# A weighted mixture kernel on one core: probabilities moved into the second product's operands, weight sums moved to other steps

## The chip, the core and the metric

The kernel runs on one core of one Trainium2 chip. The metric is device time in microseconds (us) of one execution, the median of three runs. Lower is better.

## The reference

Four sequences of 576 tokens, 8 heads of 64 columns, give 2304 tokens of 512 columns. Linear attention with an RMS norm makes `x`; a gated layer of 2048 hidden columns follows; then a mixture of four experts, which is what the change touches:

```python
p = domain_probs / (domain_probs.sum(-1, keepdims=True) + 1e-09)
for e in range(4):                       # w1[e]: 512 x 1024, w2[e]: 1024 x 512
    h = np.maximum(x @ w1[e], 0.0)
    out += p[:, e:e + 1] * (h @ w2[e])
```

## The kernel before

The first 468 us of the profiled execution are attention and the gated layer; the change leaves them alone but for the early part of the mixture's first operands. The rest is class `Second`. It walks 24 steps: three tiles of 768 tokens (tile 1, 2 and 3), and in each the eight half experts of 512 hidden columns. Step n has a first product (512 x 512 weights times 512 x 768 tokens) and a second product of the same size. fp32 is kept by splitting each operand into a rounded high part and a remainder: ScalarE (ACT) copies the high part (`split`, L158), VectorE (DVE) or GpSimd (POOL) subtracts it from the operand (L159). A product is then three matmul terms.

Each product is done on 2 x 2 blocks. The first product always, and the second from step 8 on, uses seven block products in place of eight, with sums of blocks as operands: `sumw` sums weight blocks, `sumx` tokens, `sumh` hidden values. A block product is 12 matmuls on TensorE (PE). In tile 1 weights come raw from memory (`load1`, `load2`), are split there, written to a buffer in HBM (`put_away`) and read back from it in tiles 2 and 3 (`get`); in tile 1 the second product has eight plain blocks (`second`), two block products for each of the four outputs.

`events` gives every action a time slot; one slot is one block product. Sorting by slot makes the program, and each engine runs its part strictly in order. A step has 15 slots in tile 1 and 14 later; first products of step n stand on odd slots, second products of step n-1 on even ones, so PE always has one of the two. All DMAs of this part but the middle outputs leave from one queue, SP's.

First products accumulate in two PSUM tiles, `x` and `z`. `keep` (ACT) and `add` (DVE, L267) move partial results to SBUF tiles `f`, named c11, c12, c22; the fourth block, c21, is what is left in `x` at the end. From these the second product's operands `hid` are made: in tile 1 by `hid` (ACT relu, L278, then a DVE subtraction with relu, L279), one for each c; later by `relu`, `sumh`, `oph`. Blocks of the second product are then multiplied by the token's probability and added to `acc`: in tile 1 by `weigh` (DVE multiplies out of PSUM, L324; POOL adds, L326), later by `keep_o`, `add`, `weigh_o` (ACT copies out of PSUM, DVE adds the next partial result, POOL multiplies, L352, and adds, L354). `leave` transposes finished tokens of tiles 1 and 2 on PE, one small piece in each of six later steps, in a bank of `ox`; `leave_last` does tile 3.

Of the kernel before, what the change touches and what calls it, by code (L numbers as in the profile page):

```python
# [80 lines left out]
class Second:  # L81
# [15 lines left out]
    ORDER = (0, 3, 2, 4, 5, 6, 1)  # L97
# [7 lines left out]
    def __init__(self, tc, w, acc, p_dram, w_dram, ident, out):  # L105
        self.tc, self.nc = tc, tc.nc
        self.w, self.acc, self.p_dram, self.w_dram, self.ident, self.out = w, acc, p_dram, w_dram, ident, out
        self.steps = NP * E2
        self.start = [0]
        for n in range(self.steps):  # L110
            self.start.append(self.start[-1] + (self.LONG if n <= E2 else self.SHORT))
        self.stacks = {}
        self.x, self.w1, self.w2, self.raw, self.s, self.h, self.f, self.t, self.ps, self.pb = ({} for _ in range(10))
# [16 lines left out]
    def open_left(self):  # L130
# [6 lines left out]
        self.m_p = self.open("left", "m", 2)  # L137
        self.away_p = self.open("first_left", "away", 2)
        self.s2_p = self.open("first_left", "s2", 3)
        self.raw2_p = self.open("first_left", "raw2", 4)  # L140
        self.ps2 = self.open("psum", "ps2", 1, space=PSUM)

    def change(self):

        self.stacks["first_right"].close()
        self.stacks["first_left"].close()
        self.t_p = self.open("right", "t", 6, side="right")
        self.h7_p = self.open("right", "hid7", 1, side="right")
        self.e_p = self.open("left", "e", 4)
# [124 lines left out]
    def hid(self, n, name, src):  # L274

        src = self.f[n, src] if src in ("c11", "c12", "c22") else self.of_ps(n, src)
        h = self.hid_tile(name)
        self.nc.scalar.activation(h[:, 0], src, AF.Relu)  # L278
        self.nc.vector.scalar_tensor_tensor(h[:, 1], src, 0.0, h[:, 0].bitcast(F32), op0=ALU.max, op1=ALU.subtract)  # L279
        self.h[n, name] = h  # L280

    def relu(self, n, name):
        self.nc.scalar.activation(self.f[n, name], self.f[n, name], AF.Relu)

    def sumh(self, n, name):

        f = self.t_p.tile([128, 2, HN], F32, tag="t", name="t")
        if name == "t3":
            self.nc.vector.tensor_tensor(f, self.f[n, "t2"], self.f[n, "c11"], op=ALU.subtract)
        else:  # L290
            a, b = dict(t1=("c12", "c11"), t2=("c22", "t1"), t4=("x", "t2"))[name]
            a = self.of_ps(n, a) if a == "x" else self.f[n, a]
            self.nc.vector.scalar_tensor_tensor(f, a, 0.0, self.f[n, b], op0=ALU.max, op1=ALU.subtract)
        self.f[n, name] = f

    def oph(self, n, name, eng=None):
        h = self.hid_tile(name)
        self.split(h, self.f[n, name], eng)
        self.h[n, {"c11": "b11"}.get(name, name)] = h
# [15 lines left out]
    def probs(self, n, j):  # L315
        t, q = divmod(n, E2)
        return self.pb[t, q // 2][:, j * HN : j * HN + HN].unsqueeze(1).to_broadcast([128, 2, HN])

    def weigh(self, n, b):

        i, j = self.BLOCKS[b]
        a = self.sums(0, i, j)
        m = a if n == 0 else self.m_p.tile([128, 2, HN], F32, tag="m", name="m")
        self.nc.vector.tensor_tensor(m, self.of_ps(n, b), self.probs(n, j), op=ALU.mult)  # L324
        if n:
            self.nc.gpsimd.tensor_tensor(a, a, m, op=ALU.add)  # L326
# [8 lines left out]
    def keep_o(self, n, c, name):  # L335
        t = self.e_p.tile([128, 2, HN], F32, tag="e", name="e")
        self.nc.scalar.activation(t, self.of_ps(n, c), AF.Copy)  # L337
        self.f[n, name] = t

    def weigh_o(self, n, name, c=None):  # L340

        i, j = int(name[1]) - 1, int(name[2]) - 1
        a = self.sums(n // E2, i, j)
        fresh, last = n % E2 == 0, n == self.steps - 1
        eng = self.nc.vector if last and name != "o11" else self.nc.gpsimd
        if c:
            m = a if fresh else self.e_p.tile([128, 2, HN], F32, tag="e", name="e")
            self.nc.vector.tensor_tensor(m, self.of_ps(n, c), self.probs(n, j), op=ALU.mult)  # L348
        else:
            t = self.f.pop((n, name))  # L350
            m = a if fresh else t
            eng.tensor_tensor(m, t, self.probs(n, j), op=ALU.mult)  # L352
        if not fresh:
            (self.nc.vector if last and c else eng).tensor_tensor(a, a, m, op=ALU.add)  # L354

    def leave(self, t, b):

        p = self.bank(self.ps2, 0, "t")
# [25 lines left out]
    def events(self):  # L384
# [7 lines left out]
        for n in range(self.steps):  # L392
# [17 lines left out]
            lead = self.LEAD + (2.5 if n == 0 else 0)  # L410
            for k in range(7):
# [24 lines left out]
            put(b0 + 10.5, self.hid, n, "b22", "c22")  # L436
            put(b0 + 12.1, self.add, n, "z", "c12")
            put(b0 + 12.2, self.ps.pop, (n, "z"))
            put(b0 + 14.1, self.hid, n, "b21", "x")
            if make:  # L440
                put(b0 + 4.5, self.hid, n, "b11", "c11")
                put(b0 + 12.5, self.hid, n, "b12", "c12")
                put(b0 + 14.2, self.ps.pop, (n, "x"))
                for i, name in ((4.6, "c11"), (10.6, "c22"), (12.6, "c12")):
                    put(b0 + i, self.f.pop, (n, name))

                for k, (i, j) in enumerate(((0, 0), (0, 1), (1, 0), (1, 1))):
                    put(b0 + (5.6 if n == 1 else 1) + 0.5 * k, self.load2, n, i, j)
                    put(b0 + (7.2, 8.6, 10.2, 14.7)[k] + 0.7 * (n == 1), self.op2, n, f"a{i + 1}{j + 1}", pool)
                for k, i in ((0, 10), (1, 11.5), (6, 17.2)):  # L450
                    put(b0 + i, self.put_away, n, 2, k)
                late = (9, 4)[n] if n < 2 else 0
                for name, i in (("s1", 5.2), ("s2", 5.3), ("s3", 9.2), ("s4", 11.2)):
                    put(b0 + late + i, self.sumw, n, 2, name, pool if name in ("s1", "s3") else None)
                for k, i in ((3, 5.5), (4, 9.4), (2, 11.3), (5, 13.2)):
                    i += late
                    put(b0 + i, self.op2, n, self.A[k], pool if k != 2 else None)
# [523 lines left out]
```

## Time and profile before

| | us |
|---|---|
| median of three runs (1262.45 to 1264.41) | 1262.68 |
| profiled execution | 1257.88 |
| its span, first to last instruction | 1255.4 |
| PE busy in the span | 1191.7 |

The profiled execution is 4.8 us below the median of the runs. The span is read in four stretches: 0 to 468 us (attention and gated layer), 468 to 742 (tile 1), 742 to about 1228 (tiles 2 and 3, with the change of tile at 985 to 1026), and the end. "Busy" of an engine counts its own instructions. An arrow `<-` names what ended an engine's idle time. PEclk is the granted share of TensorE's clock: 1.00 is 2.4 GHz, 0.50 is 1.2 GHz.

### The profile page before, as it was taken

To read this page: it belongs to the slowest core of one execution; us is meant where nothing else is said; L and a number is where in the kernel's file an instruction comes from. 1 tells how busy PE (TensorE), PEld (TensorE's weight loads), DVE (VectorE), ACT (ScalarE), POOL (GpSimd) and SP (SyncE) were. 2 spreads that over 40 slices of the span, in tenths; PEclk is the share of its full clock that TensorE was granted. 3 is DMA by queue.
4 is the path that set the end of the run, shared out by engine and by line. 5 is a ranking of instruction groups with operands and counts; after the bars stand their busy time and mean duration, and the time that the engine had idled before them with its cause. 6 is when DMAs were issued, how large, how long until landed. Compare 5 with 4: busy or idle time off the path is not lost.

```text
span 1255.4 us, 17061 instructions
## 1 busy us (share of the span) xinstructions
PE 1191.7 (95%) x6513; PEld 1111.5 (89%) x6513; DVE 756.1 (60%) x932; ACT 498.6 (40%) x777; POOL 579.5 (46%) x369
## 2 busy tenths in 40 slices
PE   6889999999999998999999979999999899999996
PEld 5778798888888887899999979999999899999996
DVE  4985545555653467667777764455557755555555
ACT  4555443433332244443443333333334433333333
POOL 2563433302300034577766753255556553555553
PEclk9999999999999999999999999999999999999999
DMA  9523011201200028787878666888888678878863
GB/s 331 194 72 110 22 63 51 67 1 52 67 1 1 1 84 288 265 310 283 299 266 296 234 236 233 262 262 260 268 262 253 228 236 258 262 264 262 263 203 100
DMA packets 85235, 234.48 MB, mean 187 GB/s; under 512 B 10204, under 2 KB 32804, under 8 KB 85156
## 3 DMA queue, kind: packets, MB, share of 16 engines
q1 hardware_dynamic: 83140, 230.23, 54.8%
q10 hardware_dynamic: 2016, 3.18, 0.7%
q8 instruction: 51, 0.84, 0.3%
q14 instruction: 28, 0.23, 0.1%
HBM read 169.91 MB, written 63.48 MB: 186 GB/s over the span
## 4 chain that ended last, share of the span: by engine, by line
PE 64%; DVE 9%; issue 5%; ACT 3%; POOL 2%; DMA 2%; SPq 2%; DVEq 0%; POOLq 0%; ACTq 0%
PE a L831 12%; PE p_h L793 12%; PE ps_x L249 12%; PE ps_ox L249 9%; PE ps_z L249 8%; PE ps_oz L249 7%; PE ps_o L312 4%; DVE w L159 2%; DVE f L267 2%; DVE s L200 1%; ACT hid L278 1%; DMA raw<-in_w 1%; SPq L183 1%; ACT w L158 1%; POOL w L159 1%
## 5 line engine op out<-in xcount | busy, mean ns | idle before, releaser
L249 PE MATMUL ps_x<-x,w 128*128 128x384 f32 x1152 | 217.1, 336 | 2.4 <-DVE f L267 2.4
L249 PEld LDWEIGHTS ps_x<-x,w 128*128 128x128 f32 x1152 | 203.1, 189 | 2.8 <-DVE f L267 2.7
L312 PE MATMUL ps_o<-hid,w 128*128 128x384 f32 x768 | 152.5, 347 | 20.3 <-ACT hid L278 20.2
L249 PE MATMUL ps_z<-x,w 128*128 128x384 f32 x864 | 163.3, 337 | 4.3 <-issue 2.2
L312 PEld LDWEIGHTS ps_o<-hid,w 128*128 128x128 f32 x768 | 139.3, 195 | 24.6 <-ACT hid L278 22.8
L249 PEld LDWEIGHTS ps_z<-x,w 128*128 128x128 f32 x864 | 151.7, 189 | 6.5 <-issue 3.3
L249 PE MATMUL ps_ox<-hid,w 128*128 128x384 f32 x768 | 145.4, 337 | 5.3 <-ACT e L337 5.3
L249 PEld LDWEIGHTS ps_ox<-hid,w 128*128 128x128 f32 x768 | 135.1, 189 | 6.2 <-ACT e L337 6.2
L793 PE MATMUL p_h<-x_hi,w_hi 128*128 128x512 f32 (+1 forms) x320 | 119.9, 375 | 1.1 <-ACT o L729 1.1
L653 POOL TENSOR_TENSOR cv_a<-wd_raw,cv_a 128x512 f32<-128x512 f32 x28 | 37.6, 1341 | 180.4 <-ACT sg L807 71.2
L793 PE MATMUL p_h<-x_lo,w_hi 128*128 128x512 f32 (+1 forms) x320 | 119.1, 372 | 0.5 <-DVE x_lo L779 0.5
L831 PE MATMUL a<-h_lo,w_hi 128*128 128x512 f32 (+1 forms) x320 | 118.3, 370 | 1.1 <-DVE h_lo L817 1.1
L793 PE MATMUL p_h<-x_hi,w_lo 128*128 128x512 f32 (+1 forms) x320 | 119.0, 372 | 0.0
L831 PE MATMUL a<-h_hi,w_hi 128*128 128x512 f32 (+1 forms) x320 | 118.5, 370 | 0.0
L831 PE MATMUL a<-h_hi,w_lo 128*128 128x512 f32 (+1 forms) x320 | 118.0, 369 | 0.0
L352 POOL TENSOR_TENSOR e<-e,pb 128x768 f32<-128x768 f32 x40 | 75.1, 1877 | 85.0 <-DVE e L267 85.0
L354 POOL TENSOR_TENSOR acc<-acc,e 128x768 f32<-128x768 f32 x53 | 99.8, 1884 | 24.3 <-DVE e L348 21.1
L808 DVE TENSOR_TENSOR sg<-p_h,sg 128x512 f32<-128x512 f32 (+1 forms) x80 | 50.8, 637 | 99.9 <-ACT sg L807 99.6
L249 PE MATMUL ps_oz<-hid,w 128*128 128x384 f32 x576 | 108.5, 336 | 0.0
L159 POOL TENSOR_TENSOR hid<-t,hid 128x768 fp32r<-128x768 f32 x32 | 59.9, 1872 | 95.3 <-ACT hid L158 95.3
L807 ACT ACTIVATE sg<-p_h 128x512 f32<-128x512 f32 (+1 forms) x80 | 44.4, 555 | 146.6 <-PE p_h L793 139.2
L249 PEld LDWEIGHTS ps_oz<-hid,w 128*128 128x128 f32 x576 | 100.3, 188 | 0.2 <-DVE e L267 0.2
(145 smaller groups left out, 2012.1 us busy)
## 6 DMA issues: line engine op xcount, KB each, us to landing
w<-w_dram SPq DMA_DIRECT2D x224, 512.0 KB, 4.3
w_dram<-w SPq DMA_DIRECT2D x112, 512.0 KB, 3.7
raw<-in_w SPq DMA_DIRECT2D x128, 128.0 KB, 3.5
wd_raw<-in_wd SPq DMA_DIRECT2D x28, 512.0 KB, 3.8
pb<-p_dram SPq DMA_DIRECT2D x12, 384.0 KB, 5.4
kv_first_lo<-in_kv SPq DMA_DIRECT2D x6, 512.0 KB, 10.3
q_raw<-in_qt SPq DMA_DIRECT2D x6, 512.0 KB, 7.1
out<-o ACTq DMA_DIRECT2D x12, 256.0 KB, 3.1
```

What stands on the lines that cost most here:

```text
L158: self.nc.scalar.activation(t[:, 0], f, AF.Copy)
L159: (eng or self.nc.vector).tensor_tensor(t[:, 1], f, t[:, 0].bitcast(F32), op=ALU.subtract)
L249: self.nc.tensor.matmul(p[:, f, :HN], w[0][:, a, c : c + 128], x[:, b, kp, :], start=self.FRESH[k] and a == b == kp == 0, stop=b == kp == ...
L267: self.nc.vector.tensor_tensor(t, self.of_ps(n, c), t, op=ALU.add)
L312: self.nc.tensor.matmul(o, w[:, u, c : c + 128], h[:, v, kp, :], start=m == 0, stop=m == 11)
L352: eng.tensor_tensor(m, t, self.probs(n, j), op=ALU.mult)
L354: (self.nc.vector if last and c else eng).tensor_tensor(a, a, m, op=ALU.add)
L653: nc.gpsimd.tensor_tensor(a, l, a, op=ALU.mult)
L793: nc.tensor.matmul(p[:, :n], wt[:, 0, cols], xt[:, kc, :], start=k == 0, stop=k == 3 * KC - 1)
L807: nc.scalar.activation(sg[:, :n], p[:, :n], AF.Sigmoid)
L808: nc.vector.tensor_tensor(sg[:, :n], p[:, :n], sg[:, :n], op=ALU.mult)
L831: nc.tensor.matmul(o, a, m, start=first and k == 0, stop=last and k == 2)
```

## The change

Relu and probability become one DVE instruction on the hidden block, `max` with 0 and `mult` by the probability, before anything is summed or split. Since the second product is linear, its blocks then need no weight, and `gather` adds each from PSUM to `acc` in one DVE instruction (the first time a tile's block is touched, ACT copies instead). `weigh`, `keep_o`, `weigh_o` and `hid` go.

```diff
-    ORDER = (0, 3, 2, 4, 5, 6, 1)
+    ORDER = (0, 3, 2, 5, 4, 1, 6)
+    GATHER = (("ox", 0, 0), ("oz", 1, 1), ("ox", 0, 1), ("oz", 0, 1), ("ox", 1, 1), ("oz", 0, 0), ("ox", 1, 0))
     def relu(self, n, name):
-        self.nc.scalar.activation(self.f[n, name], self.f[n, name], AF.Relu)
+        if name == "c21":
+            self.f[n, name] = self.f_p.tile([128, 2, HN], F32, tag="f", name="f")
+        f = self.f[n, name]
+        src = self.of_ps(n, "x") if name == "c21" else f
+        self.nc.vector.scalar_tensor_tensor(f, src, 0.0, self.probs(n, int(name[2]) - 1), op0=ALU.max, op1=ALU.mult)
+    def gather(self, n, k, i, j):
+        a = self.sums(n // E2, i, j)
+        if (n, i, j) not in self.begun and n % E2 == 0:
+            self.nc.scalar.activation(a, self.of_ps(n, k), AF.Copy)
+            self.begun.add((n, i, j))
+        else:
+            self.nc.vector.tensor_tensor(a, self.of_ps(n, k), a, op=ALU.add)
     def again(self, n, k):
-                self.ps[n, "o" + c] = self.bank(self.ps2, i, "o" + c)
+                self.ps[n, "o" + c] = self.bank(self.ps2, n + i, "o" + c)
     def leave(...):
-        p = self.bank(self.ps2, 0, "t")
+        p = self.bank(self.ps2, n + 1, "t")
```

The sums of second weights (s1 to s4 of each half expert) leave the step that uses the raw blocks. Half expert n's are now made in steps 2n and 2n+1, two in each, so over tiles 1 and 2, from blocks that are loaded a second time (pool `raw3`), and all on DVE:

```diff
+        for n in range(E2):
+            a, b = self.start[2 * n] + (7 if n == 0 else 0), self.start[2 * n + 1] + (3 if n == 0 else 0)
+            for k, (i, j) in enumerate(((1, 0), (1, 1), (0, 0), (0, 1))):
+                put(a + 0.4 + 0.1 * k, self.load2, n, i, j, True)
+            for at, name in ((a, "s1"), (a + 2, "s2"), (b, "s3"), (b + 2, "s4")):
+                put(at + 5.5, self.sumw, n, 3, name)
+                put(at + 7.3, self.op2, n, name)
+                put(at + 9.2, self.put_away, n, 2, k)
```

Further: `op1` of k 4 goes to POOL and `op2` of a12 to DVE; step 1's first operands are made two slots later; token operands 0 and 1 of tiles 2 and 3 are split on POOL; the probabilities are loaded before the step, not in it; the last outputs leave in another order. The kernel's matmuls are the same in number and size.

A step of tile 1 on DVE, from the last addition to c22 (from `ps_x`) to the operand made of c12; `w` and `s` are weight operands and sums, `m` a weighted block. Before:

```order
L267 TENSOR_TENSOR f<-ps_x,f 128x768
L200 TENSOR_TENSOR s<-raw_4857,raw_4866 128x512
L200 TENSOR_TENSOR s<-s,raw_4885 128x512
L279 SCALAR_TENSOR_TENSOR hid<-f,hid 128x768
L324 TENSOR_TENSOR m<-ps_o,pb 128x768
L200 TENSOR_TENSOR s<-raw_4839,s 128x512
L159 TENSOR_TENSOR w_5052<-s,w_5052 128x512
L159 TENSOR_TENSOR w_5070<-s,w_5070 128x512
L267 TENSOR_TENSOR f<-ps_z,f 128x768
L279 SCALAR_TENSOR_TENSOR hid<-f,hid 128x768
```

Now:

```order
L269 TENSOR_TENSOR f<-ps_x,f 128x768
L202 TENSOR_TENSOR s<-raw_5466,raw_5472 128x512
L286 SCALAR_TENSOR_TENSOR f<-f,pb 128x768
L202 TENSOR_TENSOR s<-s,raw_5491 128x512
L160 TENSOR_TENSOR hid<-f,hid 128x768
L307 TENSOR_TENSOR acc<-ps_o,acc 128x2x384
L160 TENSOR_TENSOR w_5676<-s,w_5676 128x512
L269 TENSOR_TENSOR f<-ps_z,f 128x768
L286 SCALAR_TENSOR_TENSOR f<-f,pb 128x768
L160 TENSOR_TENSOR hid<-f,hid 128x768
```

One weight sum and one weight operand left the stretch, and a relu with probability entered before each of the two `hid` subtractions.

The end of the program on PE, from the last first product (into `ps_x`) on; `ps_t` are the last output's transposes. Before:

```order
L249 MATMUL ps_x<-x_8630,w_10495 128x384 x12
L249 MATMUL ps_ox<-hid,w_10511 128x384 x12
L249 MATMUL ps_oz<-hid,w_10542 128x384 x12
L249 MATMUL ps_ox<-hid,w_10573 128x384 x12
L249 MATMUL ps_ox<-hid,w_10606 128x384 x12
L249 MATMUL ps_oz<-hid,w_10653 128x384 x12
L249 MATMUL ps_ox<-hid,w_10679 128x384 x12
L376 MATMUL ps_t<-ident,acc 128x128 x6
L249 MATMUL ps_oz<-hid,w_10695 128x384 x12
L376 MATMUL ps_t<-ident,acc 128x128 x18
```

Now:

```order
L251 MATMUL ps_x<-x_8714,w_10478 128x384 x12
L251 MATMUL ps_ox<-hid,w_10499 128x384 x12
L251 MATMUL ps_oz<-hid,w_10528 128x384 x12
L251 MATMUL ps_ox<-hid,w_10557 128x384 x12
L251 MATMUL ps_oz<-hid,w_10589 128x384 x12
L251 MATMUL ps_ox<-hid,w_10627 128x384 x12
L350 MATMUL ps_t<-ident,acc 128x128 x6
L251 MATMUL ps_oz<-hid,w_10654 128x384 x12
L350 MATMUL ps_t<-ident,acc 128x128 x6
L251 MATMUL ps_ox<-hid,w_10672 128x384 x12
L350 MATMUL ps_t<-ident,acc 128x128 x12
```

`ox` and `oz` now strictly alternate, and three of the four groups of transposes stand apart instead of in a row at the end.

## Rows read from the trace of the kernel before

**Rows 1.** Stretches: length, busy us by engine (instructions), clock, DMA share, GB/s.

```profile
468.00:742.00 274.00, 249.69 (x1367) 243.47 (x1366) 194.36 (x181) 109.79 (x175) 181.57 (x113) 0.97 0.77 275
742.00:985.00 243.00, 241.87 (x1391) 240.50 (x1391) 135.43 (x134) 93.19 (x119) 121.34 (x65) 1.00 0.80 258
```

**Rows 2.** PE's waits from 486 to 742 us: total, times, longest.

```profile
PE ps_o L312 <- ACT hid L278: 20.2, 8, 5.1
PE ps_x L249 <- DVE f L267: 2.4, 1, 2.4
PE ps_z L249 <- ACT f L262: 1.5, 1, 1.5
```

**Rows 3.** PE's waits from 742 to 1216 us.

```profile
PE ps_t L362 <- DVE e L348: 2.3, 6, 0.4
PE ps_z L249 <- issue: 2.2, 1, 2.2
PE ps_ox L249 <- ACT e L337: 1.9, 1, 1.9
```

**Rows 4.** Stretches behind two of PE's waits, columns as in rows 1.

```profile
491.20:494.60 3.40, 3.01 (x9) 3.01 (x10) 3.03 (x4) 2.60 (x5) 1.24 (x2) 0.50 0.40 160
...
999.80:1003.20 3.40, 3.40 (x13) 3.40 (x12) 0.96 (x1) 0.16 (x1) 0.28 (x1) 0.50 0.20 65
```

**Rows 5.** DVE's timeline, step 4 of tile 1: start, us, instruction [idle before].

```profile
619.52 0.96 DVE L267 TENSOR_TENSOR f<-ps_x,f 128x768 f32<-128x768 f32 x1 [2.88 <-PE ps_x L249]
620.39 0.68 DVE L200 TENSOR_TENSOR s<-raw,raw 128x512 f32<-128x512 f32 x1
621.11 1.76 DVE L200 TENSOR_TENSOR s<-s,raw 128x512 f32<-128x512 f32 x1
622.79 2.05 DVE L279 SCALAR_TENSOR_TENSOR hid<-f,hid 128x768 fp32r<-128x768 f32 x1
624.77 0.95 DVE L324 TENSOR_TENSOR m<-ps_o,pb 128x768 f32<-128x768 f32 x1
625.64 0.91 DVE L200 TENSOR_TENSOR s<-raw,s 128x512 f32<-128x512 f32 x1
626.47 2.94 DVE L159 TENSOR_TENSOR w<-s,w 128x512 fp32r<-128x512 f32 x2
629.33 0.95 DVE L267 TENSOR_TENSOR f<-ps_z,f 128x768 f32<-128x768 f32 x1
```

**Rows 6.** POOL's timeline of the same stretch.

```profile
621.03 1.29 POOL L159 TENSOR_TENSOR w<-s,w 128x512 fp32r<-128x512 f32 x1 [0.74 <-ACT w L158]
622.29 3.72 POOL L159 TENSOR_TENSOR w<-raw,w 128x512 fp32r<-128x512 f32 x2
625.96 2.30 POOL L326 TENSOR_TENSOR acc<-acc,m 128x768 f32<-128x768 f32 x1
```

**Rows 7.** The end of that stretch on ACT and on PE.

```profile
630.31 0.84 ACT L278 ACTIVATE hid<-f 128x768 fp32r<-128x768 f32 x1 [6.54 <-DVE f L267]
...
631.21 2.66 PE L312 MATMUL ps_o<-hid,w 128*128 128x384 f32 x12 [1.38 <-ACT hid L278]
```

**Rows 8.** DVE by shape from 742 to 1216 us: busy, mean ns | idle before.

```profile
L267 DVE TENSOR_TENSOR f<-ps_z,f 128x768 f32<-128x768 f32 x31 | 29.5, 952 | 49.8 <-PE ps_z L249 49.8
...
L289 DVE TENSOR_TENSOR t<-t,f 128x768 f32<-128x768 f32 x15 | 14.3, 952 | 0.0
```

**Rows 9.** The end of the span on PE and ACT, timeline.

```profile
1226.93 2.24 PE L249 MATMUL ps_ox<-hid,w 128*128 128x384 f32 x12
...
1229.02 2.25 PE L249 MATMUL ps_oz<-hid,w 128*128 128x384 f32 x12
...
1233.65 2.38 PE L249 MATMUL ps_ox<-hid,w 128*128 128x384 f32 x12 [2.39 <-ACT e L337]
...
1250.15 0.85 PE L376 MATMUL ps_t<-ident,acc 128*128 128x128 f32 x6 [1.01 <-ACT o L378]
...
1251.03 0.81 ACT L378 ACTIVATE o<-ps_t 128x768 f32<-128x768 f32 x1 [0.99 <-PE ps_t L376]
```

More of the change, by code (lines that the diff above doesn't have):

```diff
@@ L272, in hid_tile, with probs @@
         return self.h_p.tile([128, 2, 2, HN], F32R, tag="hid", name="hid")
[L274 to L280, printed above, removed]
-    def relu(self, n, name):
-        self.nc.scalar.activation(self.f[n, name], self.f[n, name], AF.Relu)
+    def probs(self, n, j):
+        t, q = divmod(n, E2)
+        return self.pb[t, q // 2][:, j * HN : j * HN + HN].unsqueeze(1).to_broadcast([128, 2, HN])
+    def relu(self, n, name):
+        if name == "c21":
[3 more added lines that the diff above has]
+        self.nc.vector.scalar_tensor_tensor(f, src, 0.0, self.probs(n, int(name[2]) - 1), op0=ALU.max, op1=ALU.mult)
     def sumh(self, n, name):
         f = self.t_p.tile([128, 2, HN], F32, tag="t", name="t")
[L288 to L293, printed above, removed]
+        a, b = dict(t1=("c12", "c11"), t2=("c22", "t1"), t3=("t2", "c11"), t4=("c21", "t2"))[name]
+        self.nc.vector.tensor_tensor(f, self.f[n, a], self.f[n, b], op=ALU.subtract)
         self.f[n, name] = f
@@ L313, in second @@
                 m += 1
[L315 to L326, printed above, removed]
     def again(self, n, k):
@@ L331, in again, with leave @@
             for i, c in enumerate("xz"):
-                self.ps[n, "o" + c] = self.bank(self.ps2, i, "o" + c)
+                self.ps[n, "o" + c] = self.bank(self.ps2, n + i, "o" + c)
         self.product(self.ps[n, "o" + self.INTO[k]], (self.w2.pop((n, k)), 2), self.h.pop((n, self.B[k])), k)
[L335 to L356, printed above, removed]
-        p = self.bank(self.ps2, 0, "t")
+    def leave(self, n, t, b):
+        p = self.bank(self.ps2, n + 1, "t")
         for k in range(2):
@@ L435, in events @@
             put(b0 + 10.1, self.add, n, "x", "c22")
-            put(b0 + 10.5, self.hid, n, "b22", "c22")
             put(b0 + 12.1, self.add, n, "z", "c12")
             put(b0 + 12.2, self.ps.pop, (n, "z"))
-            put(b0 + 14.1, self.hid, n, "b21", "x")
+            put(b0 + 4.3, self.relu, n, "c11")
+            put(b0 + 5.3, self.oph, n, "c11")
+            put(b0 + 10.3, self.relu, n, "c22")
+            put(b0 + (10.5 if n else 12.55), self.oph, n, "c22", None if make else pool)
+            put(b0 + 12.25, self.relu, n, "c12")
@@ L440, in events @@
+            put(b0 + 14.05, self.relu, n, "c21")
+            put(b0 + 14.06, self.ps.pop, (n, "x"))
             if make:
[L441 to L444, printed above, removed]
+                put(b0 + 12.5, self.oph, n, "c12")
+                put(b0 + 14.1, self.oph, n, "c21")
+                for i, name in ((5.4, "c11"), (12.6, "c22"), (12.6, "c12"), (14.2, "c21")):
@@ L453, in events @@
[L453 to L457, printed above, removed]
-                    put(b0 + i + 0.01, self.raw.pop, (n, 2, self.A[k]))
-                    put(b0 + i + 1.8, self.put_away, n, 2, k)
-                    put(b0 + i + 1.81, self.w2.pop, (n, self.A[k]))
@@ L461, in events @@
-                for k in ("a11", "a12", "a21", "a22"):
-                    put(b0 + max(11.45 + late, 15.45 if k == "a22" else 0), self.raw.pop, (n, 2, k))
+                    at = b0 + ((7.2, 8.6, 10.2, 14.7) if n else (7.2, 8.6, 15.2, 17.7))[k]
+                    put(at - 5.5, self.load2, n, i, j)
+                    put(at, self.op2, n, f"a{i + 1}{j + 1}", pool if k != 1 else None)
+                    put(at + 0.01, self.raw.pop, (n, 2, f"a{i + 1}{j + 1}"))
+                    if k != 2:
+                        put(at + 2.5, self.put_away, n, 2, (0, 1, None, 6)[k])
@@ L465, in events @@
                         put(after + 4 * b + 2 * d, self.second, n, b, d)
-                    put(after + 4 * b + 3.2, self.weigh, n, b)
+                    put(after + 4 * b + 3.2, self.gather, n, b, *self.BLOCKS[b])
                     put(after + 4 * b + 3.21, self.ps.pop, (n, b))
```

108 lines of the change are left out of this document (48 added, 60 removed).

## The prediction

> **What bounds the kernel now.** I read the busy times by stretch first. From 742 to 985 us PE is busy 241.87 of 243.00 us, from 468 to 742 only 249.69 of 274.00 [rows 1]. The change leaves the matmuls as they are, so what it can win is PE's idle time and the time at the lower clock, and most of that lies in tile 1. Second, PE's waits. In tile 1 there are ten, 20.2 + 2.4 + 1.5 = 24.1 us, and eight of them, one a step, stand before a step's first block of the second product, until ACT has made the high part of `hid` [rows 2]. In tiles 2 and 3 PE waits six times for a free bank for `leave`, 2.3 us, and 2.2 + 1.9 us where tile 3 takes over [rows 3]. Third, the clock: in a stretch of 3.4 us the granted share is 0.50 (1.2 GHz) behind the first of these waits, and the same behind the change of tile [rows 4]; the first and the last of six such stretches stand there, five in tile 1. Each costs 3.4 x 0.5 = 1.7 us of PE's work. The wait of 1.38 us in rows 7 is not followed by one.
>
> Why is ACT late with `hid`? Rows 5 to 7 show it for step 4, and I count from DVE's start there (619.52). ACT only copies what DVE has added last, at 629.33; it starts at 630.31 and PE at 631.21 [rows 5, 7]. PE had waited 1.38 us, so the block was due at 631.21 - 1.38 - 619.52 = 10.3. DVE is not idle in between, it works off eight instructions. With spacings where nothing disturbs them, 0.87 us for 768 columns (619.52 to 620.39) and 0.72 for 512 (620.39 to 621.11), the add on c12 would start at 3 x 0.87 + 5 x 0.72 = 6.2 and not at 9.8. The 3.6 us are POOL's: it works 1.29 + 3.72 + 2.30 = 7.3 us there [rows 6], and DVE instructions with both inputs in SBUF take 1.76 in place of 0.68 and 2.05 in place of 0.96, about 1.1 us more each, while the one that reads PSUM keeps its 0.95 [rows 5].
>
> **Tile 1.** By the order, a usual step's DVE instructions go from 23 to 28, POOL's from 15 to 6. The new relu with probability reads two SBUF inputs; its nearest row is a DVE instruction of that shape, 0.952, and the new `gather` is an addition out of PSUM like that of c11, 0.952 too [rows 8]. The added DVE work hides under PE if it is done when its product is due, so I walk the new queue of the same stretch, with the same spacings. Add c22 0.87, sum 1.59, relu 2.46, sum 3.18; the high part of c22 waits for relu's end (2.55) and ACT's 0.84 [rows 7], so its subtraction starts at 3.4 and the gather at 4.3; weight operand 5.2, add c12 at 5.9. The add and the relu that needs its result take 0.96 each, so ACT starts at 7.8, and PE can start at 8.7 (0.90 from ACT to PE, [rows 7]). Due: 10.3. So 1.6 us are spare before POOL's disturbance. Of POOL's work the adds and a third of the weight operands are gone; two weight operands of 1.29 each remain in this stretch, 2.6 us for 7.3. Scaled, they cost 3.6 x 2.6 / 7.3 = 1.3: PE could start at 10.0, just in time. The bounds are no disturbance (8.7) and the whole of the old one (12.3, a wait of 2.0). I take 10.0, since it is worked out from the same stretch.
>
> In step 0 no second products stand between, and c12's block is one product (2.08 us, [rows 9]) from its turn: add 0.97, relu 0.98, ACT to PE 0.9 and 0.3 from PE to DVE make 3.1, so about 1.0 stays, with 0.3 for c22's remainder behind it: 1.3 for the 5.1 of now. In step 7 sums and splits of tile 2's tokens enter the queue (four more DVE instructions of 0.95); I leave 0.6 there. So of 24.1 us there stay 1.9, and 22.2 are won. No wait is left that is as long as those before the lower clock, so five stretches, 5 x 1.7 = 8.5, go too.
>
> **Weight sums.** Two sums and two operands a step, all on DVE, are in the 28 above. In tile 2 they are new: 26 DVE instructions in place of 16, and 22 in place of 16 in tile 3, with 3 on POOL in place of 9. For tile 2 that is 22 x 0.87 + 4 x 0.72 = 22.0 us of a step of 14 x 2.08 = 29.2; three waits for ACT of 0.9 and three POOL instructions at 1.1 make 28.0. It fits, with 1.2 us to spare, and every product has slots in hand: t1's high part is ready 0.3 + 3 x 0.9 + 0.9 = 3.9 us after c12's product, and due four slots, 8.3 us, after it. I cost it at nothing; the cover is PE's own work, and beyond 29.2 each us is a us per step. The second loading and the late `put_away` add 4 x 128 KB and 2 x 512 KB a step, 1.5 MB in 29.2 us = 54 GB/s to the 258 of now [rows 1]. On SP's queue `put_away` waits for DVE two slots after its operand's turn, with `get`s behind it that run eight slots ahead.
>
> **Leave and the change of tile.** `leave` takes the bank of `oz`, whose gather is due a slot before: its 2.3 us [rows 3] go. At the change of tile DVE's list grows from 21 to 30 instructions in step 15, POOL's shrinks from 10 to 5, and c21 now needs one DVE instruction before `x` is free where it needed three steps on DVE and ACT. The wait of 4.1 and one low stretch of 1.7 could all go, or all stay; I take half, 2.9.
>
> **The end.** From the last step's first block, at 1226.93 [rows 9], all seven follow one another. In the new order DVE does relu c21, a gather, t2's remainder, two sums, and only then the second gather, ending at 7.5; the fourth block reuses that bank and was due at 6.25, so 1.3 us are lost. From 7.5 on: four blocks (8.3) and two of the transposes (0.85 each, [rows 9]) end at 17.6, the last gather at 18.9, transposes at 19.8, ACT starts at 19.9. Now it starts at 1251.03 - 1226.93 = 24.1 [rows 9], the wait of 2.39 included. 4.2 us are won; 3.0 if t4's remainder on POOL is late, 5.5 if the gather isn't.
>
> **The sum.** 22.2 + 8.5 + 2.3 + 2.9 + 4.2 = 40.1 us. The profiled execution's 1257.9 would become 1217.8; the median of the runs is 4.8 above it, 1262.7 - 40.1 = 1222.6, so 1223. With all bounds at their best 24.1 + 8.5 + 2.3 + 5.8 + 5.5 = 46.2: 1216.5.
>
> **The rivals.**
> POOL blocks. If a DVE instruction that meets POOL stood still until POOL's ended, two POOL instructions would cost 2 x 1.29 = 2.6 for my 1.3, PE would start at 11.3 and wait 1.0 in six steps, without a fall of the clock: 1223 + 6 = 1229. Against it: in rows 6 POOL's instructions are longer as well (1.86 mean in the pair for 1.29 alone), so both are slowed. The Trainium skill has this as a rule ("SBUF — State Buffer", Who interferes with whom): an exclusive lock, where the later one fully blocks, if DVE has two SBUF inputs. By the rule 1229; the trace agrees on which instructions are hit and has both stretched.
>
> The disturbance stays. If DVE's six SBUF-only instructions of the stretch lose the whole 3.6 us, the wait is 2.0 in seven steps, with the low clock behind most. Then step 0's 3.8 + 1.7, `leave`, half the change of tile and the end remain, 14.9: 1248. For it: the new relu adds SBUF inputs. Against it: POOL's nine instructions fewer.
>
> DMA binds in tile 2. The share 0.80 at 258 GB/s [rows 1] becomes 0.97 at 312. If 300 is all that goes, each of eight steps takes 29.2 x 12 / 300 = 1.2 us more: 1232. Tile 1 has moved 275 at 0.77, which makes room beyond 312.
>
> DVE becomes the clock of tiles 2 and 3: slower. Its queue now has eleven instructions a step that wait for PE, seven of them gathers. If each leaves 0.4 us idle that the next can't use, 28.0 + 4.4 = 32.4, 3.2 us beyond PE's 29.2, in 15 steps 48 us: 1223 + 48 = 1271. It decides against the change from 29.2 + 40.1 / 15 = 31.9 on. Against it: DVE stands 49.8 us before the additions out of `ps_z` alone [rows 8], in tiles where PE hardly waits; spare time is there.
>
> Nothing moves: another wait, raw blocks that come late to DVE's sums say, holds PE as `hid` did. 1262.
>
> **How the numbers follow.** Forecast 0.55, blocks 0.13, disturbance stays 0.15, DMA 0.08, slower 0.06, nothing 0.03. The range reaches from the best bounds, a us below 1216.5, to the disturbance's 1248: 1215 to 1248, which leaves out some 0.15 to 0.2. A measurement of this kernel can tell 0.2%, 2.5 us, from no change. Faster 0.91, within 0.2% 0.03, slower 0.06.
>
> **What would show it.** Right: PE's waits before the first second block of a step under 0.5 us from step 1 on; no stretch at 0.50 in tile 1; DVE's SBUF-only instructions near 0.95 and 0.69; no `leave` wait; ACT's last copy some 20 us behind the last step's first block. Wrong: waits of 2 us that stay, with DVE instructions of 1.7 and 2.0 in front; PE's waits in tile 2 or 3 behind a gather or a weight sum; a DMA share near 1 in tile 2 with PE waiting for `w`.

## The result and the profile after

The changed kernel takes 1220.0 us (median of four runs, 1216.2 to 1221.5) against 1262.7 for the kernel before beside it: a ratio of 0.9655, 95% interval 0.963 to 0.968. Two later measurements on other chips gave 0.9647 (0.9625 to 0.9669) and 0.9662 (0.9637 to 0.9686). The profiled execution took 1216.2 us, span 1214.4; before it was 1257.9 and 1255.4. So the span shrank by 41.0 us.

Where they went, from the starts of four of PE's instructions in either trace: up to the first second block of tile 1 2.9 us, from there to the end of step 7's second product (the first `ps_ox`) 29.0, tiles 2 and 3 6.2, from the last step's first block on 2.9.

The stretches of the changed kernel, columns as in [rows 1]: length, busy us of PE, weight load, DVE, ACT, POOL with instructions, clock, DMA share, GB/s.

```profile
468.00:732.00 264.00, 262.06 (x1495) 259.25 (x1494) 201.42 (x233) 112.30 (x173) 75.33 (x51) 1.00 0.84 297
732.00:970.00 238.00, 234.89 (x1358) 233.88 (x1356) 194.48 (x202) 81.13 (x108) 50.72 (x27) 1.00 0.89 304
```

In tile 1 PE idles 1.9 of 264 us where it idled 24.3 of 274 [rows 1], POOL works 75 us for 182, and the clock is 1.00 throughout. PE's waits, first from 486 to 740 us (answering [rows 2]), then from 740 to 1190 ([rows 3]), then at the end:

```profile
PE ps_o L320 <- ACT hid L159: 1.2, 1, 1.2
PE ps_x L251 <- ACT f L264: 0.5, 1, 0.5
...
PE ps_x L251 <- ACT f L264: 2.6, 1, 2.6
PE ps_oz L251 <- issue: 1.9, 1, 1.9
...
PE ps_oz L251 <- DVE acc L307: 1.1, 1, 1.1
```

The first line of [rows 2], eight waits for `hid`, has become one wait, in step 0. The six for `leave` are gone. At the change of tile two waits stand, 4.5 us together for the 4.1 of the two before. And the step of tile 1 that the prediction walked, on DVE and then ACT ([rows 5, 7]):

```profile
605.26 0.96 DVE L269 TENSOR_TENSOR f<-ps_x,f 128x768 f32<-128x768 f32 x1 [1.40 <-PE ps_x L251]
606.13 0.68 DVE L202 TENSOR_TENSOR s<-raw,raw 128x512 f32<-128x512 f32 x1
606.74 0.95 DVE L286 SCALAR_TENSOR_TENSOR f<-f,pb 128x768 f32<-128x768 f32 x1
607.61 0.68 DVE L202 TENSOR_TENSOR s<-s,raw 128x512 f32<-128x512 f32 x1
608.60 0.96 DVE L160 TENSOR_TENSOR hid<-f,hid 128x768 fp32r<-128x768 f32 x1 [0.31 <-ACT hid L159]
609.48 0.95 DVE L307 TENSOR_TENSOR acc<-ps_o,acc 128x768 f32<-128x768 f32 x1
610.34 0.68 DVE L160 TENSOR_TENSOR w<-s,w 128x512 fp32r<-128x512 f32 x1
610.94 0.95 DVE L269 TENSOR_TENSOR f<-ps_z,f 128x768 f32<-128x768 f32 x1
611.92 0.96 DVE L286 SCALAR_TENSOR_TENSOR f<-f,pb 128x768 f32<-128x768 f32 x1
...
612.98 0.85 ACT L159 ACTIVATE hid<-f 128x768 fp32r<-128x768 f32 x1 [3.88 <-DVE f L286]
```

ACT starts 7.7 us behind the addition on c22 (the walk said 7.8), and no DVE instruction of this step is longer than its undisturbed time.

### The profile page after: what moved, and what is told of

It reads as the page before. It is cut to its first block, busy times and chain, and to the rows that moved or that the text cites. A ratio compares the mean times of both kernels' runs of the same rounds, so it can differ in the third digit from the quotient of the medians.

```text
span 1214.4 us, 17105 instructions
## 1 busy us (share of the span) xinstructions
PE 1177.3 (97%) x6513; PEld 1103.0 (91%) x6513; DVE 836.8 (69%) x1081; ACT 459.9 (38%) x725; POOL 308.3 (25%) x219
## 4 chain that ended last, share of the span: by engine, by line
PE 78%; DVE 6%; ACT 1%; issue 1%; DMA 0%; ACTq 0%; DVEq 0%
PE ps_x L251 14%; PE a L802 13%; PE p_h L764 12%; PE ps_z L251 11%; PE ps_o L320 10%; PE ps_ox L251 9%; PE ps_oz L251 7%; DVE f L286 1%; DVE hid L160 1%; DVE t L292 1%; ACT hid L159 1%; DVE acc L307 1%; DVE f L269 1%; DVE s L202 1%; PE ps_t L336 0%
## 5 line engine op out<-in xcount | busy, mean ns | idle before, releaser
L159 ACT ACTIVATE hid<-f 128x768 fp32r<-128x768 f32 x80 | 67.5, 845 | 213.2 <-DVE f L286 213.2
L320 PE MATMUL ps_o<-hid,w 128*128 128x384 f32 x768 | 143.4, 335 | 1.4 <-ACT hid L159 1.2
L320 PEld LDWEIGHTS ps_o<-hid,w 128*128 128x128 f32 x768 | 133.9, 188 | 2.6 <-ACT hid L159 1.6
L159 ACT ACTIVATE hid<-t 128x768 fp32r<-128x768 f32 x64 | 54.0, 843 | 124.0 <-DVE t L292 124.0
L160 POOL TENSOR_TENSOR w<-raw,w 128x512 fp32r<-128x512 f32 x41 | 57.9, 1419 | 161.6 <-ACT w L159 89.3
```

The costliest lines, as they stand in the source:

```text
L159: self.nc.scalar.activation(t[:, 0], f, AF.Copy)
L160: (eng or self.nc.vector).tensor_tensor(t[:, 1], f, t[:, 0].bitcast(F32), op=ALU.subtract)
L320: self.nc.tensor.matmul(o, w[:, u, c : c + 128], h[:, v, kp, :], start=m == 0, stop=m == 11)
```

## The experiments

Each of these is one edit, most of them of the changed kernel. Where only a profile was taken, it is one execution, set against 1216 to 1220 for the three profiled executions of the changed kernel. Durations such as "34.2 us a step" are from PE's starts of one block in two steps.

**Only the probability fold** (the second part undone), sums_back:

```diff
-        for n in range(E2):
...
+                for name, i in (("s1", 5.2), ("s2", 5.3), ("s3", 9.2), ("s4", 11.2)):
+                    put(b0 + late + i, self.sumw, n, 2, name, pool if name in ("s1", "s3") else None)
+                for k, i in ((3, 5.5), (4, 9.4), (2, 11.3), (5, 13.2)):
+                    put(b0 + late + i, self.op2, n, self.A[k], pool if k != 2 else None)
```

> The changed kernel with its second part undone: the sums of second weights are made again in the step that uses the raw blocks, from one loading, on the old engines and slots (also a12's operand back on POOL). The probability fold stays. Theory A (each part took its share of DVE's queue ahead of c12, and POOL's work holds DVE up): between the add on c22 and the operand of c12 DVE has one more weight sum or operand than in the changed kernel, twelve instructions; undisturbed the walk is add 0.87, sum 1.59, relu 2.46, sum 3.18, remainder 3.4 to 4.3, gather 5.15, sum 5.87, two operands 7.3, add and relu 9.2, PE 10.1, due 10.3. POOL has about four weight operations of 1.29 there again, which cost DVE between 1.3 and the 3.6 that they cost in the kernel before: PE's waits before the first second block come back, 1.1 to 3.4 us in each of steps 1 to 7, some with a stretch at clock 0.50 behind; the profiled execution goes from 1216 to 1225 to 1240. Theory B (the fold alone did it, the sums' place does not matter): waits in tile 1 stay under 0.5 us a step, 1216 to 1219.

Measured: 1251.9 us. PE's waits from 486 to 760 us, then DVE and POOL in one step:

```profile
PE ps_o L319 <- ACT hid L158: 18.7, 8, 3.3
PE ps_x L250 <- DVE f L268: 6.2, 2, 3.8
PE ps_z L250 <- ACT f L263: 2.5, 2, 2.2
```

```profile
626.66 0.96 DVE L268 TENSOR_TENSOR f<-ps_x,f 128x768 f32<-128x768 f32 x1 [3.89 <-PE ps_x L250]
627.54 1.50 DVE L201 TENSOR_TENSOR s<-raw,raw 128x512 f32<-128x512 f32 x1
628.96 2.05 DVE L285 SCALAR_TENSOR_TENSOR f<-f,pb 128x768 f32<-128x768 f32 x1
630.93 1.78 DVE L201 TENSOR_TENSOR s<-s,raw 128x512 f32<-128x512 f32 x1
...
627.19 1.30 POOL L159 TENSOR_TENSOR w<-s,w 128x512 fp32r<-128x512 f32 x1 [0.74 <-ACT w L158]
628.44 3.72 POOL L159 TENSOR_TENSOR w<-raw,w 128x512 fp32r<-128x512 f32 x2
```

Theory A, and worse than the 1225 to 1240 that it gave. Three DVE instructions lose 3 us to three of POOL's weight operations, and the block behind them comes 2.1 us late. DVE had been idle 3.89 us just before: its list as a whole is short enough, the part between c22 and c12 is not. In tile 1 the fold alone wins nothing: 27.4 us of waits stand there, for the 24.1 of [rows 2].

**Only the moved sums**, before_spread. This kernel makes the sums of half experts 0 to 3 alone. It leaves out those that the changed kernel makes in tile 2, and tiles 2 and 3 read the four half experts' sums twice:

```diff
-                for name, i in (("s1", 5.2), ("s2", 5.3), ("s3", 9.2), ("s4", 11.2)):
-                    put(b0 + late + i, self.sumw, n, 2, name, pool if name in ("s1", "s3") else None)
...
+        for n in range(4):
+            a, b = self.start[2 * n] + (7 if n == 0 else 0), self.start[2 * n + 1] + (3 if n == 0 else 0)
...
+            for at, name in ((a, "s1"), (a + 2, "s2"), (b, "s3"), (b + 2, "s4")):
...
+                put(at + 5.5, self.sumw, n, 3, name)
+                put(at + 7.3, self.op2, n, name)
```

> The kernel before with the second part alone, in tile 1: two weight sums and two operands a step, on DVE, from blocks loaded a second time. For want of room only half experts 0 to 3 get their sums so, tiles 2 and 3 read those of n mod 4 (same loads, other numbers); raw2 has two buffers. Theory A (DVE's queue ahead of c12): add 0.87, two sums 2.31, remainder 3.18, weighing 4.05, operand 4.8, add on c12, ACT 0.98 after its start, PE 0.90 later: 6.7 undisturbed; with all of the old disturbance of 3.6 from POOL 10.3, which is when the block is due. So the waits before the first second block go from 1.3 to 5.1 us a step to under 0.5 in steps 1 to 7, without the fold: tile 1 gives 16 of its 20 us and most of its low clock, 1257.9 to about 1233 to 1240. Theory B (the fold is what frees tile 1): the waits stay within a third of the old ones, 1250 to 1258.

Measured: 1223.1 us. Its only wait from 486 to 742 us:

```profile
PE ps_o L314 <- ACT hid L280: 2.3, 1, 2.3
```

Theory A, and further than expected: moving the weight sums alone takes 35 of the 41 us. POOL's additions are still there (1.8 to 2.3 us each). In the step from 604.8 us one of them starts at the end of the stretch between c22 and c12, and lengthens nothing in it. What the rest of the change adds is in tiles 2 and 3, 452.5 us here against 448.4, and at the end, 29.1 against 25.5. The moved sums do two things at once. They shorten DVE's list in that stretch, and they take five operations a step off POOL (40 in four steps of 31.25 us, 10 a step, for the 15 before). No run separates the two in the kernel before.

**Useless work on POOL in tile 1**, as much as before (pool_load), then in its two halves, the additions behind each gather (pool_adds) and the five subtractions at fixed slots (pool_weights); `pad` is a tile of zeros:

```diff
+    def more(self, block=None):
+        if block is None:
+            self.nc.gpsimd.tensor_tensor(self.pad, self.pad, self.pad, op=ALU.subtract)
+        else:
+            a = self.sums(0, *block)
+            self.nc.gpsimd.tensor_tensor(a, a, self.pad[:, :HN].unsqueeze(1).to_broadcast([128, 2, HN]), op=ALU.add)
...
+                    put(after + 4 * b + 3.2, self.more, self.BLOCKS[b])
+                for k in (5.2, 5.5, 9.2, 9.4, 13.2):
+                    put(b0 + k, self.more)
```

> The changed kernel with useless work on POOL in tile 1, as much as the kernel before had there: each step four additions of zero to an acc block behind its gather (768 columns) and five subtractions of 512 columns. DVE's queue is that of the changed kernel. Theory A (POOL's operations and DVE's with two SBUF inputs take turns, so POOL's work itself made DVE late): DVE's instructions with two SBUF inputs are again 1.7 to 2.9 us long; in the stretch ahead of c12 they lose up to 3.6, PE could start at 8.6 + 3.6 = 12.2 against a due time of 10.3: waits of 0.5 to 2 us in steps 1 to 7, 4 to 14 us in all, and 1.7 for each fall of the clock: 1220 to 1238. Theory B (DVE's shorter queue decides, POOL only fills gaps): waits stay under 0.5 us a step, 1216 to 1219.

> The changed kernel with the first half of pool_load's useless work alone: POOL adds zero to an acc block behind each gather of tile 1 (768 columns, 4 a step). In pool_load nine operations lengthened DVE's work by 7.9 us a step (25.5 to 33.4), 0.88 each, and DVE with its waits for ACT (3.9) was then the clock of the step, 35.5 us. Theory A (a sum: DVE's list plus 0.9 to 1.1 for each of POOL's operations, against PE's 31.2): 25.5 + 4.0 + 3.9 = 33.4, so PE waits up to 2 us a step: 1224 to 1236. Theory B (only what meets DVE between c22 and c12 counts; one addition does, 8.6 + 1.6 = 10.2 of 10.3): no waits, 1216 to 1220.

> The changed kernel with the other half alone: five subtractions of 512 columns a step on POOL in tile 1, as many as the weight sums and operands that the change took from it. Theory A (the sum): 25.5 + 5 x 0.88 + 3.9 = 33.8 against 31.2, waits up to 2.5 us a step: 1224 to 1238. Theory B (the stretch between c22 and c12): in it POOL ran 3.4 us of weight work in pool_load, so 8.6 + 1.3 to 3.4 = 9.9 to 12.0 of 10.3, waits 0 to 1.7 a step: 1216 to 1230. Neither half alone giving waits would mean that only both together make DVE the clock.

Measured: 1258.0, 1245.8 and 1230.0 us. DVE's list is the changed kernel's in all three. Four steps of the changed kernel, then of pool_weights, pool_adds and pool_load, columns as above:

```profile
550.00:675.00 125.00, 125.00 (x722) 125.00 (x721) 96.44 (x114) 51.26 (x80) 34.28 (x24) 1.00 0.85 302
```

```profile
567.00:692.00 125.00, 124.90 (x712) 122.88 (x711) 109.24 (x112) 51.40 (x80) 69.74 (x44) 1.00 0.82 289
```

```profile
567.00:692.00 125.00, 118.99 (x670) 117.39 (x669) 110.52 (x101) 48.78 (x76) 72.35 (x39) 0.99 0.76 269
```

```profile
567.00:709.00 142.00, 132.60 (x720) 130.67 (x720) 127.13 (x112) 51.26 (x80) 103.59 (x61) 0.95 0.72 258
```

And DVE's waits in the first and the last of these stretches (total, times, longest):

```profile
DVE hid L160 <- ACT hid L159: 12.5, 16, 1.0
DVE f L269 <- PE ps_x L251: 5.6, 4, 1.4
DVE acc L307 <- PE ps_o L320: 3.7, 4, 0.9
...
```

```profile
DVE hid L162 <- ACT hid L161: 12.4, 16, 1.0
DVE w L162 <- ACT w L161: 3.0, 4, 0.7
```

Taken over whole steps, from one addition on c22 to the next, DVE is busy 24.1 us a step in the changed kernel (96.44 / 4), and 27.8, 30.1 and 31.8 in the others. The waits for ACT, (12.4 + 3.0) / 4 = 3.9, make that 28.0, 31.7, 34.0 and 35.7. PE's own step is 15 x 2.08 = 31.2. Steps lasted 31.2, 31.7, 34.2 and 35.7 us. That sum and step agree is bookkeeping, since in the three loaded kernels DVE has next to no other idle time. The finding is only this: DVE hardly waits for PE any more, so its list, as POOL lengthens it, is the length of the step. In pool_weights this is half a us beyond PE's own step. PE loses it where a weight load waits for `hid` (24 matmuls from 621.89 take 4.80 us for 4.33), which the list of PE's waits does not show. The changed kernel's DVE waits 9.3 / 4 = 2.3 us a step for PE, and has 3.2 to spare by the sum.

Theory A of the sum holds, but not with one price. A 512-column operation cost 3.7 / 5 = 0.7 us. An addition of 768 columns, which starts behind a `gather` and lengthened one DVE instruction each time in the step that I read, cost 6.0 / 4 = 1.5. Together they cost 7.7 and not 9.7, so the prices do not simply add up. The run that decides between the theories is pool_adds: theory B allowed it no waits, and it lies beyond theory A's 1236 too, as pool_load lies beyond 1238. The 1230 of pool_weights fit both. So the rule "one addition between c22 and c12 fits" was wrong.

Part of these times is not the load. In all three PE waits 3.0 to 3.9 us in step 0, ahead of the first added operation, for 1.2 in the changed kernel. POOL's one clearing of `pad`, at 478.0 us in pool_weights, waits 7.2 us for DVE, and the weight operands behind it come late. This takes some 3.6 us of pool_weights and of pool_load, and 4.5 of pool_adds. At the edges of tile 1 pool_weights also waits 2.4 us in step 1, and 1.3 and 2.2 in step 7.

**DVE's slack in tile 3**, dve_load (`more` subtracts a tile of 768 columns in SBUF from itself on DVE):

```diff
+            extra = (4, 4, 8, 8, 12, 12)[n - 17] if 17 <= n <= 22 else 0
+            for k in range(extra):
+                put(b0 + 14 * (k + 0.5) / extra + 0.037, self.more)
```

> The changed kernel with useless subtractions on DVE in tile 3, 768 columns, two inputs from SBUF, evenly over the step: 4 a step in steps 17 and 18, 8 in 19 and 20, 12 in 21 and 22. A step of PE is 29.2 us there; DVE's own 22 instructions, three waits for ACT and three meetings with POOL make some 25. Theory A (DVE has slack that it can use; it becomes the clock only when its list is longer than PE's): 4 x 0.87 = 3.5 more is 28.6, no wait of PE; 8 give 32, 2.8 us a step lost; 12 give 35.5, 6.3 a step; in all 18 us, 1216 to 1234. Rival B (each of the seven gathers and four partial sums waits for PE and leaves idle time that the next cannot use): PE waits already with 4, 2 to 4 us a step, 8 and 12 lose 7 and 10: some 40 us, 1256.

Measured: 1228.6 us. A stretch of a step each with 4, 8 and 12 more, then PE's waits from 1100 to 1190 us:

```profile
1011.20:1040.00 28.80, 28.80 (x171) 28.76 (x170) 23.61 (x25) 8.63 (x12) 6.82 (x3) 1.00 0.82 252
...
1069.50:1098.50 29.00, 29.00 (x170) 29.00 (x169) 27.95 (x29) 8.67 (x12) 6.35 (x3) 1.00 0.83 265
...
1128.00:1158.00 30.00, 26.56 (x148) 25.10 (x147) 28.93 (x31) 7.17 (x10) 5.52 (x3) 1.00 0.66 208
```

```profile
PE ps_oz L259 <- issue: 3.0, 2, 1.5
PE ps_oz L259 <- DVE acc L315: 2.9, 4, 1.1
...
```

No wait with 4, none with 8, where DVE is busy 27.95 of 29.00 us; some 3.5 us a step with 12. In tile 3 the rival is gone, and theory A was too cautious as well. It put DVE's list at 25 us with three waits for ACT; the changed kernel's tile 3 has 123.55 x 29.2 / 179 = 20.2 busy, some 23 with these waits of 0.9.

**DMA in tile 3**, dma_load (`more` reads 512 KB into a spare tile):

```diff
+            extra = (2, 2, 4, 4, 6, 6)[n - 17] if 17 <= n <= 22 else 0
+            for k in range(extra):
+                put(b0 + 14 * (k + 0.5) / extra + 0.037, self.more, n, k)
```

> The changed kernel with useless reads from HBM of 512 KB each in tile 3, on the same queue: 2 a step in steps 17 and 18, 4 in 19 and 20, 6 in 21 and 22. 14 reads a step move 251 GB/s at a share of 0.79 there, tile 2 moves 304 at 0.89; with 2, 4 and 6 more PE's pace would ask for 287, 323 and 359. Theory A (the share rises by some 0.1 for 53 GB/s, so it reaches 1 near 360): no wait with 2 and 4, at most 1 us a step with 6: 1216 to 1219. Rival B (about 300 GB/s is all that goes): with 4 a step takes 18 x 0.524 / 0.300 = 31.4, 2.2 more than 29.2, with 6 34.9, 5.7 more: 16 us in all, 1232.

Measured: 1217.5 us, and in tile 3 PE waits nowhere. Stretches of a step each with 2, 4 and 6 more reads:

```profile
1011.20:1040.00 28.80, 28.80 (x170) 28.76 (x170) 19.32 (x22) 9.83 (x13) 5.56 (x3) 1.00 0.86 283
1040.00:1069.50 29.50, 29.50 (x175) 29.46 (x174) 20.05 (x22) 8.73 (x12) 5.58 (x3) 1.00 0.97 339
...
1098.50:1128.00 29.50, 29.50 (x172) 29.50 (x172) 20.01 (x23) 9.22 (x12) 5.04 (x3) 1.00 0.99 369
```

At 369 GB/s and a share of 0.99 PE loses nothing: a read lands after 6.6 us (median) for 4.3, and `get` runs eight slots, 16.6 us, ahead. The rival's 300 GB/s is not a limit here. The Trainium skill ("Perfetto Trace Analysis", Engine Utilization and Roofline) gives 358 GB/s as a core's share of the memory and says that a lone core can pull more; the 369 agree.

**Another order at the places that still wait**, e_order, e_order2, e_order3. At 953 us and near the end the cause is the order of DVE's list alone. At 953 us a `gather` stands behind a subtraction that waits for ACT:

```profile
951.74 0.96 DVE L160 TENSOR_TENSOR hid<-t,hid 128x768 fp32r<-128x768 f32 x1 [0.97 <-ACT hid L159]
952.62 0.95 DVE L307 TENSOR_TENSOR acc<-ps_ox,acc 128x768 f32<-128x768 f32 x1
```

Near the end it stands behind two sums, none of them lengthened. At 971 us the order and a meeting with POOL come together, here in the changed kernel on DVE, POOL, ACT and PE:

```profile
967.09 2.60 DVE L233 TENSOR_TENSOR t<-acc 128x768 f32<-128x768 f32 x1
...
966.99 1.88 POOL L160 TENSOR_TENSOR hid<-t,hid 128x768 fp32r<-128x768 f32 x1 [4.42 <-ACT hid L159]
...
969.73 0.84 ACT L159 ACTIVATE x<-t 128x768 fp32r<-128x768 f32 x1 [2.81 <-DVE t L233]
970.47 0.79 ACT L264 ACTIVATE f<-ps_x 128x768 f32<-128x768 f32 x1
...
971.32 0.97 PE L251 MATMUL ps_x<-x,w 128*128 128x384 f32 x4 [2.55 <-ACT f L264]
```

DVE's token sum starts 0.1 us after POOL's subtraction and ends 0.82 us after its end; ACT's copy out of `ps_x` stands behind the split that needs that sum. The edit of e_order3 against the changed kernel (`end` is 2.01 and `late` 1.85 in the last step, else 0; `at` are the slots of the token splits, and the sum t3 goes to 3.25):

```diff
+                if t == 2:
+                    at[4], at[5] = b0 + 4.35, b0 + 6.5
...
-                put(after + 1.16, self.sumh, n, "t4")
+                put(after + end + 1.16, self.sumh, n, "t4")
...
-                put(after + 3.3, self.oph, n, "c21")
+                put(after + late + 3.3, self.oph, n, "c21")
...
-                    put(after + 2 * m + (1.1 if m < 6 else 0.45), self.gather, n, *g)
+                    put(after + 2 * m + (1.1 if m < 6 else 0.35), self.gather, n, *g)
```

> The changed kernel with three places of its order mended. (1) The last gather of a step in tiles 2 and 3 comes 0.1 slot earlier, ahead of t1's subtraction, which waits for ACT: the wait of 1.88 us at 953.67 should go. (2) The split of tile 3's t3 comes 0.7 slot later, so ACT copies c12 out of ps_x before it waits for that sum: the wait of 2.55 us at 971.32 should go. (3) In the last step two sums stand behind the gather out of ps_oz: the wait of 1.10 us near the end should go. Theory A: all three waits are of the order alone: 5.5 us, 1216.2 to 1211 for a profiled execution at the same clock, median 1214 to 1215. Rival B: DVE and ACT are only late there because POOL holds up DVE's token sums; then (1) and (2) move to the next block and under 2 us are won, median 1218 to 1220.

> The changed kernel itself, for comparison on the same chip with the next ones: 1216 to 1222, its waits where they were (1.2 in step 0, 1.9 and 2.6 at the change of tile, 1.1 near the end).

> The changed kernel with another order at three places. The last gather of a step ahead of t1's subtraction, as in e_order (its wait of 1.88 went there). At the change to tile 3 the sum t3 of the new tokens is made at slot 3.25, where DVE stood idle 1.4 us, and its split follows at 4.35, ahead of the long sum that stood in front of it (2.59 us beside POOL); the split of the fourth token block comes 0.35 slot later, so that POOL does not meet the subtraction for c21. In the last step only the sum t4 moves behind the gather out of ps_oz, so POOL's remainder for t3 is not late as it was in e_order. Theory A (each of these waits is DVE's order or a meeting with POOL): of 1.88 + 2.55 + 1.10 = 5.5 us at most 0.7 stay, profiled 1211 to 1212, median 5 below the changed kernel's on this chip. Theory B (the next instruction is as late as the one moved): as in e_order, 4.7 of waits stay, under 2 us won.

> The changed kernel once more, beside e_order3 on the same chip: waits of 9.0 us in the mixture, 1216 to 1221.

> e_order2 with two more moves. At the change to tile 3 the split of the fourth token block (POOL's remainder) goes to slot 6.5, so that POOL no longer meets the subtraction for c21 (2.60 us there in e_order2, and the next addition 1.0 us late). In the last step the operand of c21 is made after the third gather, which stood behind its subtraction (2.52 us beside POOL) and held PE 1.94 us. Theory (a meeting of POOL with one DVE subtraction is what each of these waits is): 1.00 + 0.37 + 1.94 go, some 2.5 us of waits stay in the mixture (1.9 of them in step 0) for 9.0 in the changed kernel: profiled 6.5 us less at the same clock, median 5 to 7 below the changed kernel's on this chip. Rival (the meeting only moves to the next subtraction): over 4.5 us of waits stay, median under 3 below.

Measured: e_order 1217.2 us (ratio to before 0.9665, 0.9644 to 0.9686, no gain that can be told from the changed kernel's 0.9655); e_order2 1215.5 (1214.0 to 1216.7) beside the changed kernel's 1217.4 (1215.9 to 1220.5), 2 us that the runs hardly tell apart; e_order3 **1210.2** (1207.3 to 1211.6) beside the changed kernel's 1217.5 (1215.5 to 1220.4) on the same chip, 7 us, ratio to before 0.9607 (0.9586 to 0.9628).

Only the wait at 953 us went at the first try. The other two came back one instruction later, as rival B had said of (1) and (2). It was (2) and (3). PE's waits in e_order at the end and at the change of tile:

```profile
PE ps_ox L251 <- issue: 2.4, 1, 2.4
PE ps_x L251 <- ACT x L159: 1.9, 1, 1.9
```

In e_order2, at the end on DVE:

```profile
1194.15 2.52 DVE L160 TENSOR_TENSOR hid<-f,hid 128x768 fp32r<-128x768 f32 x1
1196.60 0.94 DVE L307 TENSOR_TENSOR acc<-ps_ox,acc 128x768 f32<-128x768 f32 x1
```

POOL works from 1193.47 on two remainders, the subtraction for c21 takes 2.52 us beside them, and the gather behind it lets PE wait 1.9. e_order3 puts the gather ahead of that subtraction and, at the change of tile, takes POOL's split out of the way of DVE's subtraction for c21. All waits of 0.1 us and more that PE has left from 486 us to the end of the span:

```profile
PE ps_o L320 <- ACT hid L159: 1.2, 1, 1.2
PE ps_x L251 <- ACT f L264: 0.5, 1, 0.5
PE ps_t L350 <- DVE acc L307: 0.5, 1, 0.5
PE ps_o L320 <- DVE hid L160: 0.2, 1, 0.2
```

## Why the prediction was right, and where it was not

- **Tile 1's waits**, 22.2 predicted: 24.1 - 1.7 = 22.4. Step 0 was put at 1.3 and kept 1.2; step 7's 0.6 did not come. The walk held to 0.1 us in its undisturbed part. The term for POOL, 1.3 us, was right in steps 1 and 2, where the relu takes 2.04 us (513.21) and a sum 1.72 (543.64) beside POOL, 1.4 and 1.0 us lost in the stretch. In steps 3 to 6 it was 0. There POOL's two weight operations run from 603.6 to 606.3, beside the addition on c22, which reads PSUM, and the next only at 617.8. No block waited, since 8.6 and 10.0 both lie under the 10.3 that are due.
- **The low clock**, 5 x 1.7 = 8.5: all five stretches are gone.
- **What of the change did it.** The step "POOL's adds and a third of its weight operands are gone" named POOL rightly (pool_load gives as much back with DVE's new list, some 3.6 us of it by clearing `pad`), but did not ask which part was needed. Without the fold, tile 1 is as free (before_spread, one wait); without the moved sums it isn't free at all (sums_back). The adds hold PE up with DVE's list of 28 (pool_adds) and not with one of 24 (before_spread).
- **Leave**, 2.3: gave 3.7. From one of its pieces to the next PE takes 30.1 us for 30.7, 0.6 less six times, more than the listed waits of 0.4.
- **Change of tile**, 2.9 by taking half: the mis-sized term. The waits stayed, 1.9 + 2.6 = 4.5 for 4.1, and the low stretch of 1.7 went. From the last piece of `leave` in tile 2 to the first in tile 3 PE's starts give 184.0 - 181.3 - 0.6 = 2.1. That the low stretch went is luck: in the profile of after_again, the same kernel, the clock is 0.50 from 972.7 to 976.0 us, behind the same waits. The reason given, fewer instructions on POOL and one step for c21, was not what PE waited for. It was a gather behind a subtraction that waits for ACT, of the order alone (e_order), and ACT's copy behind a token sum that POOL held up (e_order3).
- **The end**, 4.2: ACT's last copy starts 1209.54 - 1188.87 = 20.7 us behind the last step's first block, for 24.1 [rows 9] and the predicted 19.9: 3.4, of which 2.9 reach the end of the span. The late second gather cost 1.1 as foreseen (1.3); 1.2 us in short waits of 0.2 to 0.5 were not foreseen.
- **The sum** came within 1 us of 41.0, in part by luck, with errors of both signs. Tile 1 gave 31.9 for 30.7 and `leave` 1.4 more than its term, the change of tile and the end 2.1 less than theirs. By the medians of the runs 42.7 us were won, for 40.1.
- **Rival "POOL blocks".** The reading against it was wrong. "Both are slowed" is what turns look like: which one comes second waits. In the changed kernel DVE's end at 969.69 is 0.82 behind POOL's, near the 0.87 that an undisturbed one takes from start to start. [Rows 5, 6] show the same: the sum ends at 622.87, 0.55 behind POOL's 622.32. The Trainium skill's rule ("SBUF — State Buffer", Who interferes with whom) holds here. The rival's 6 us did not come because the stretch meets POOL only in steps 1 and 2, within the 1.6 us that were spare.
- **Rival "DMA binds"**: 0.97 at 312 GB/s was expected, 0.89 at 304 came, and 369 did no harm.
- **Rival "DVE becomes the clock"**: DVE was put at 28.0 us of a step of tile 2, 2.7 of them waits for ACT; it is busy 194.48 x 29.2 / 238 = 23.9, so some 26.6 with them. Gathers that wait for PE don't lose their idle time: in tile 3 dve_load fills a step to 27.95 of 29.00. In tile 1 the rival is nearer than the prediction saw, 2.3 to 3.2 us a step.

## What to carry to other kernels

When a matmul waits for a copy, list what the engine behind it has to do between the last input and the due time, and move work out of that stretch; here that alone was worth 35 of 41 us. Where two engines take turns, as DVE with two inputs in SBUF and POOL do here, ask of each operation of the slower one which of the other's it will meet: the same four additions cost PE nothing beside a list of 24 instructions and 3 us a step beside one of 28. When the last waits are a few, look at the order of each list there, and at what the moved instruction will meet in its new place: two of three such waits came back one instruction later.

## What the runs showed of the hardware

DVE and POOL take turns. I took every DVE instruction of 512 or 768 columns with its inputs in SBUF that was lengthened by over 0.15 us, in both kernels and in sums_back, before_spread, pool_adds and pool_load (66 and 45 of them in the kernel before). Each ends 0.54 to 0.56 us (512) or 0.81 to 0.83 (768) after the end of a POOL instruction. One of 768 columns that reads PSUM keeps its 0.95. With DVE's list as the changed kernel has it, four POOL additions a step cost DVE 1.5 us each, five 512-column operations 0.7 each, and all nine together 7.7. In all kernels whose tile 1 has PE's waits under 0.6 us from step 1 to step 6 there is no stretch at 0.50 there. Which of the longer waits brings one was not tried: in pool_adds one of 2.2 us did at 598 us, and two as long, at 667 and 701, did not. One core moved 363 GB/s over two steps, in slices up to 422, with PE at full pace.
